# A second block of the first expert moved from the loop to the stretch between attention and loop

## Chip, core and metric

The kernel runs on one core of a Trainium2 chip. The metric is the device time of one execution in microseconds. TensorE (PE) multiplies, ScalarE (ACT) and VectorE (DVE) work elementwise, GpSimd (POOL) does elementwise work and issues indirect DMAs, SyncE (SP) issues the other DMAs. Every engine works through its own instructions in order and waits on semaphores for the others.

## The reference

```
attn: q, k, v (8, 8, 576, 64); k and v are averaged over runs of 8 rows (72 left)
      out = softmax(q kp^T / sqrt(64)) vp
x     = attn as (4608 tokens, 512)
moe:  expert = argmax(x @ w_gate) of 8; p = softmax probability of that expert
      y[token] = p * (relu(x @ w1[expert]) @ w2[expert]),  w1 512x1024, w2 1024x512
```

The tokens are grouped by their expert, each expert's tokens go through its two matrices, and the rows go back to their places.

## The kernel before

**Attention in units.** The 4608 tokens are 36 units of 128 tokens. Each unit is transposed, multiplied, exponentiated and normalised; units form seven groups (6, 6, 6, 6, 6, 4, 2). When a group is done, `route` finds each token's expert and its place in an array in HBM, `x_by_expert`, which has one segment per expert. POOL then scatters the rows there, one indirect DMA for each unit (`scatter`). The lists `hooks` and `fillers`, written by hand, say what other work is put between the steps of which unit.

**Blocks of the experts.** An expert's tokens are taken in blocks of 256 rows. All numbers are kept as pairs of fp16, a high and a low part. For one block the steps are: load the rows (`load_x`), split them into high and low (`split_x`, ACT makes the high part, DVE the low one), let the DMA transpose them into the buffer `xTs` (`turn` in two pieces, `trans` in one), copy them to `xT` on DVE (`arrive`), eight steps `up(s, f, n)` of 12 matmuls each into PSUM tiles `ps`, `ps`, `pp` (two f for each 128x512 tile), `relu_hi` (ACT) and `relu_lo` (DVE) into the buffers `bd`, four times 12 matmuls `finish(s, j, half)` into `pY[j]`, `take(j)` (ACT, times the token's probability), and `give(j)` (POOL, an indirect DMA to the output). `keep_ids`, `move_ids` and `take_ids` pass a block's token numbers and probabilities through three pairs of small buffers on POOL; `keep_ids` also overwrites the numbers in the row buffer by the mark `far`.

**The early block.** Behind the third group of units a count of the first expert's tokens is compared with 256 (`okf`). If there are that many, `early_load` at unit 29 loads the first block into `xg`; POOL splits it (`split_early` at unit 30), `turn` follows at unit 31, and the first three `up` steps are put into units 33 to 35 (`UPAT`).

**Between attention and loop.** The other `up` steps follow, and between them lie the counts of all experts (`counted`), the last group's scatters and the table of the blocks (`ended`, `table`, `tables`). `table` says for each round of the loop where its rows lie, which weight buffers it uses, and how many rounds there are (`T`). Then come `finish`, the loading and splitting of the loop's first two blocks (`xg`, `xg2`), `take` and `give`.

**The loop.** `For_i(0, T)` does one block a round (`block`). The x of the next rounds is loaded, split and transposed one and two rounds ahead. Weights of the next expert are split by ACT and DVE (`wsplit` in `part`) in the first round and in each expert's first round. Code for the four cases (weight buffers 0 or 1, 256 or 128 rows) stands one behind the other, and every engine jumps to the case that the table names.

Of the kernel before, what the change touches and what calls it, by code (L numbers as in the profile page):

```python
# [9 lines left out]
F32 = mybir.dt.float32  # L10
F16 = mybir.dt.float16
# [21 lines left out]
def kernel(  # L33
# [169 lines left out]
    for e in range(E):  # L203
# [12 lines left out]
    hT = [x.rearrange("p (f t) -> p f t", f=FC) for x in bd[0:2]]  # L216
    xh = bd[2].rearrange("p (j a x) -> p j a x", j=2, a=2)
    ys = [x.rearrange("p h d -> p (h d)") for x in ql]
    xg, xg2 = (VB[i].rearrange("p y c s x -> p (y c s x)").bitcast(F32)[:, 0:2 * XW]
               .rearrange("p (j x) -> p j x", j=2) for i in (2, 0))  # L220

    def blank_x(x):
        nc.gpsimd.memset(x, 0.0)
# [383 lines left out]
    def route(gidx):  # L607
# [103 lines left out]
        def early_pe():  # L711
            pm = psA.tile([128, 512], F32, name="pq", bufs=2)
            nc.tensor.matmul(pm[:, 0:1], ones, Z["c16"][:, 0:1], start=True, stop=True)
            V.tensor_scalar(okf, pm[:, 0:1], 256.0, None, op0=OP.is_ge)

        def early_int():
            V.tensor_copy(oki, okf[0:1, :])
# [89 lines left out]
    def put(i, pos, f, *a):  # L807
        assert 0 <= i < NU
        hooks.setdefault((i, pos), []).append((f, a))
# [94 lines left out]

    def early_load():
        assert KVS.pop("early") and not any(g < EARLY for g, _, _ in pend)
        KVS["ok"] = nc.values_load(oki[0:1, 0:1], engines=[ENG.SP], min_val=0, max_val=1)
        with tc.If(KVS["ok"] > 0):
            ld = nc.sync.dma_start(xg, xs[0:BLK, :].rearrange("(j p) x -> p j x", p=128))
        for o in scat[bounds[EARLY][0]:]:  # L910
            tc.declare_no_dep(ld.ins, o.ins, reason="rows of other tokens")
        soon.append(ld)

    put(28, "sp", blank_x, xg)
    put(29, "sp", early_load)

    def first_block():
# [102 lines left out]
    def relu_hi(k):  # L1020
        nc.scalar.activation(hT[0][:, 2 * k:2 * k + 2, :].rearrange("p f t -> p (f t)"), pH[k], AF.Relu)  # L1021
# [15 lines left out]
    pH += [pp[:, 0:512], pp[:, 512:1024]]  # L1037
    pY = [psA.tile([128, 2, 512], F32, name="po")[:, 0, :]]
    rest = [f for _, _, f in fillers]
    for x in range(max(len(front), len(rest))):  # L1040
        for f in (front[x:x + 1] + rest[x:x + 1]):
            f()
# [6 lines left out]
    def counted():  # L1049
        pc = pq["pc"] = psA.tile([128, 512], F32, name="pq", bufs=2)  # L1050
        nc.tensor.matmul(pc[:, 0:E], ones, c16, start=True, stop=True)
        rank()
        lt = pq["lt"] = work.tile([128, E], F16, name="lt")
        V.tensor_tensor(lt, pc[:, 0:E], thr, op=OP.is_gt)
        V.tensor_copy(pads, pc[0:1, 0:E])
        for x in range(2):
            h = slice(64 * x, 64 * x + 64)
            V.tensor_scalar(padi[h], pc[h, 0:E].rearrange("p (c x) -> p c x", x=2)[:, :, x], pio[h], None, op0=OP.add)
        pcs = pq["pcs"] = work.tile([128, E], F32, name="pcs")
        V.tensor_copy(pcs, pc[:, 0:E])  # L1060
        for e in range(n0 + n1):
            eng, et = ((nc.sync, ENG.SP), (nc.scalar, ENG.Activation))[e >= n0]
            r = nc.values_load(pads[0:1, e:e + 1], engines=[et], min_val=e * SEG, max_val=e * SEG + SEG - 128)
            padded.append((e, sent(eng.dma_start(xs[ds(r, 64), :], zpad[0:64]))))
# [73 lines left out]
    for f in range(FC):  # L1138
        if f >= len(UPAT):
            up(0, f, BLK)  # L1140
        if f + 1 == 5:
            counted()
        if f + 1 == 6:
            ended()
        if f + 1 == 8:
            tables()
        if f in (1, 3):
            relu_hi(f // 2)
    for k in (2, 3):
        relu_hi(k)  # L1150
    for k in range(4):
        relu_lo(k)
    views = [x.rearrange("p a b c -> p (a b c)") for x in qt] + [x.rearrange("p c x -> p (c x)")[:, 0:2048] for x in kv[1:]]
    views = [x.bitcast(F16) for x in views]
    W1[1] = [x.rearrange("p (c f) -> p c f", c=DC) for x in views[:2]]
    W2[1] = [x.rearrange("p (c f) -> p c f", c=FC) for x in views[2:]]
    pY.append(psA.tile([128, 512], F32, name="pq", bufs=2))
    for j, half in ((1, 0), (1, 1), (0, 0), (0, 1)):
        finish(0, j, half)

    def entry(kind, t, engines, lo, hi):
        ap = tabs[kind:kind + 1, t:t + 1] if isinstance(t, int) else tabs[kind:kind + 1, ds(t, 1)]
# [20 lines left out]
                with tc.If(many > 1):  # L1183
                    part(128, 64, x[0:64, 1])

    xh2 = kv[1].rearrange("p c x -> p (c x)")[:, 0:1024].bitcast(F16).rearrange("p (j a x) -> p j a x", j=2, a=2)
    blank_x(xg2)
    load_x(0)
    load_x(1, xg2)
    wlate(1)  # L1190
    for j in range(2):
        x, h = xg[:, j, 0:Dm], xh[:, j]
        nc.scalar.activation(h[:, 0], x, AF.Copy)
        V.tensor_tensor(h[:, 1], x, h[:, 0], op=OP.subtract)
    keep_ids()
    move_ids()
    turn()
    load_x(2)
    split_x(xg2, xh2)
    keep_ids(xg2)  # L1200
    trans(xh2)
    with tc.If(nc.values_load(tab[0:1, 1:2], engines=[ENG.Activation, ENG.DVE, ENG.SP], min_val=0, max_val=1) > 0):
        for j in range(8):
            wsplit(1, j)
        wwhole(2, 1)
        wwhole(3, 0)
    T = nc.values_load(tab[0:1, 0:1], min_val=1, max_val=TMAX)

    given = []

    def take(j):
# [2 lines left out]
    def give(j):  # L1214
# [6 lines left out]
            tc.declare_no_dep(st.ins, o.ins, reason="rows of other tokens")  # L1221
        given.append(st)

    take(1)
    give(1)
    take(0)
    give(0)

    def part(s, en):
        with tc.If(en > 0):  # L1230
# [76 lines left out]
```

## Time and profile before

| | us |
|---|---|
| median of 3 runs (lowest, highest) | 645.96 (644.94, 652.38) |
| profiled execution, its time | 643.61 |
| its span in the trace | 641.8 |
| PE busy | 579.4 |
| DVE, ACT, POOL busy | 335.2, 287.2, 278.2 |

The profiled execution takes 1.8 us beside its span, and it lies 2.35 us under the median of the three runs. Times in the rows below are microseconds from the start of the span. An engine's idle time stands in brackets with what released it.

### The profile page before, as it was taken

What the parts mean: (1) busy time and instruction counts of PE and PEld (TensorE: products, weight loads), DVE (VectorE), ACT (ScalarE), POOL (GpSimd) and SP (SyncE); (2) the same over time, 40 slices, a digit from 0 to 9 for tenths busy, and PEclk for the clock granted to TensorE, in tenths of its full rate; (3) what the DMA queues carried; (4) which work ended last, traced back from release to release, by engine and by line L of the source; (5) the groups of instructions that cost most, each with busy time, mean ns of one, the idle gap of its engine ahead of it and who ended that gap; (6) DMA issues with size and microseconds to landing.
All of it is one profiled execution on the core that took longest, in us unless ns stands there. A gap on an engine that the chain in (4) does not pass through costs nothing. (4 is left out here: it accounts for less than half of the span.)

```text
span 641.8 us, 15925 instructions
## 1 busy us (share of the span) xinstructions
PE 579.4 (90%) x4694; PEld 425.7 (66%) x4695; DVE 335.2 (52%) x683; ACT 287.2 (45%) x630; POOL 278.2 (43%) x531
## 2 busy tenths in 40 slices
PE   6888788888879788998899999999999989999995
PEld 5877677777758364675566677666667666677663
DVE  7577888898897417221864655213631272221212
ACT  2576676777752216221763644223622262221222
POOL 6799599798795522112125033213031232012212
PEclk9798999998989979998999999999999999999998
DMA  8997769965667774963389397633212323213200
GB/s 241 291 288 228 212 190 276 286 200 172 200 159 279 201 125 109 392 196 83 101 269 342 90 326 225 206 75 86 51 49 81 93 69 98 49 49 82 65 16 31
DMA packets 104204, 105.63 MB, mean 165 GB/s; under 512 B 62310, under 2 KB 72550, under 8 KB 104168
## 3 DMA queue, kind: packets, MB, share of 16 engines
q1 hardware_dynamic: 97528, 85.46, 47.9%
q0 software_dynamic: 6640, 19.71, 8.4%
q8 instruction: 20, 0.33, 0.2%
q14 instruction: 16, 0.13, 0.1%
HBM read 71.77 MB, written 22.06 MB: 146 GB/s over the span
## 5 line engine op out<-in xcount | busy, mean ns | idle before, releaser
L1031 PEld LDWEIGHTS <-bd 128*128 128x128 f16 x936 | 91.3, 98 | 105.7 <-ACT bd L1021 0.8
L1216 POOL TENSOR_TENSOR spacer<-ql,iG 1x1 f32<-1x1 f32 x44 | 23.8, 541 | 218.0 <-ACT ql L1212 217.0
L1025 DVE SCALAR_TENSOR_TENSOR bd<-ps,bd 128x512 f16<-128x512 f32 x44 | 30.1, 690 | 150.2 <-ACT bd L1021 150.1
L504 ACT ACTIVATE both<-ps,nmx 128x72 f32<-128x72 f32 x288 | 68.7, 325 | 32.8 <-DVE nmx L497 32.4
L1025 DVE SCALAR_TENSOR_TENSOR bd<-pp,bd 128x512 f16<-128x512 f32 x44 | 30.3, 691 | 100.6 <-ACT bd L1021 100.6
L1021 ACT ACTIVATE bd<-pp 128x512 f16<-128x512 f32 x44 | 26.2, 598 | 108.9 <-PE pp L961 78.8
L1021 ACT ACTIVATE bd<-ps 128x512 f16<-128x512 f32 x44 | 26.1, 597 | 75.8 <-PE L959 68.6
L1031 PE MATMUL po<-w,bd 128*128 128x512 f16 x264 | 58.8, 379 | 0.0
L1031 PE MATMUL po<-kv,bd 128*128 128x512 f16 x264 | 58.8, 379 | 0.0
L959 PE MATMUL ps<-kv,w 128*128 128x256 f16 (+1 forms) x176 | 44.0, 263 | 10.2 <-DMA kv<-bd 7.3
L1217 POOL DMA_INDIRECT out_dram<-ql,iG x44 | 43.8, 995 | 21.7 <-issue 20.2
L959 PE MATMUL ps<-kv,qt 128*128 128x256 f16 (+1 forms) x176 | 46.4, 268 | 4.9 <-issue 3.5
L487 PE MATMUL ps<-bd,qT 128*128 128x144 f32 x256 | 47.9, 314 | 3.2 <-DMA bd<-bd 1.6
L545 PE MATMUL po<-vb,ph 128*128 128x146 f16 (+2 forms) x384 | 33.7, 233 | 18.1 <-DVE l L586 7.3
L1031 PE MATMUL pq<-kv,bd 128*128 128x512 f16 x216 | 48.1, 379 | 0.0
L961 PE MATMUL ps<-kv,qt 128*128 128x256 f16 (+1 forms) x176 | 46.4, 268 | 1.9 <-DVE qt L116 1.9
L960 PE MATMUL ps<-kv,qt 128*128 128x256 f16 (+1 forms) x176 | 46.4, 268 | 0.0
L961 PE MATMUL ps<-kv,w 128*128 128x256 f16 (+1 forms) x176 | 44.0, 263 | 2.5 <-DVE w L116 2.5
L959 PEld LDWEIGHTS <-w 128*128 128x128 f16 x352 | 34.7, 99 | 15.7 <-issue 10.4
L960 PE MATMUL pp<-kv,qt 128*128 128x256 f16 (+1 forms) x176 | 44.7, 263 | 0.0
L961 PE MATMUL pp<-kv,qt 128*128 128x256 f16 (+1 forms) x176 | 44.7, 263 | 0.0
L959 PE MATMUL pp<-kv,qt 128*128 128x256 f16 (+1 forms) x176 | 44.7, 263 | 0.0
(235 smaller groups left out, 1374.6 us busy)
## 6 DMA issues: line engine op xcount, KB each, us to landing
both<-in_moe_w_dram SPq DMA_DIRECT2D x6, 2048.0 KB, 11.1
st<-in_moe_w_dram SPq DMA_DIRECT2D x6, 2048.0 KB, 13.4
vb<-x_by_expert SPq DMA_DIRECT2D x17, 514.0 KB
st<-in_moe_w_dram SPq DMA_DIRECT2D x8, 1024.0 KB
kv<-in_k_dram SPq DMA_DIRECT2D x7, 1024.0 KB
kv<-in_v_dram SPq DMA_DIRECT2D x7, 1024.0 KB
qt<-in_q_dram SPq DMA_DIRECT2D x6, 1024.0 KB
qt<-in_q_dram SPq DMA_DIRECT2D x4, 512.0 KB
```

Source lines behind the costliest of these rows:

```text
L487: nc.tensor.matmul(ps[:, x * 2 * KP:(x + 1) * 2 * KP], t[:, h, :], BD[b % 3][:, :, h, :], start=True, stop=True)
L504: nc.scalar.activation(p[:, h * KP:(h + 1) * KP], ps[:, x * KP:(x + 1) * KP], AF.Exp, bias=nmx[:, x:x + 1], scale=-1.0)
L545: nc.tensor.matmul(po[:, half, cols], a[:, c * 128:(c + 1) * 128], VB[b % 3][:, y, c, sl, 0:CW], start=st, stop=False, skip_group_check=True)
L959: nc.tensor.matmul(dst, wh, xT[:, d, 0:n], start=(d == 0), stop=False)
L960: nc.tensor.matmul(dst, wh, xT[:, DC + d, 0:n], start=False, stop=False)
L961: nc.tensor.matmul(dst, wl, xT[:, d, 0:n], start=False, stop=(d == DC - 1))
L1021: nc.scalar.activation(hT[0][:, 2 * k:2 * k + 2, :].rearrange("p f t -> p (f t)"), pH[k], AF.Relu)
L1025: V.scalar_tensor_tensor(l, pH[k], 0.0, h, op0=OP.max, op1=OP.subtract)
L1031: nc.tensor.matmul(y, hT[x][:, f, 128 * j:128 * j + 128], W2[s][z][:, f, :], start=(half == x == z == f == 0), stop=(half == z == 1 and f ...
L1216: nc.gpsimd.tensor_tensor(spacer[:, 0:1], ys[j][0:1, 0:1], iG[0:1, j:j + 1].bitcast(F32), op=OP.add)
L1217: st = nc.gpsimd.indirect_dma_start(out=out, out_offset=bass.IndirectOffsetOnAxis(ap=iG[:, j:j + 1], axis=0), in_=ys[j], in_offset=None, b ...
```

## The change

A second block of 256 rows of the first expert is worked through ahead of the loop.

- `early_pe` adds a comparison with 512, so that `okf` is 0, 1 or 2; the table starts at that block and the loop runs that many rounds fewer.
- `xg2` and its split `xh2` are both put into `kv[1]`. `early_load` makes two guarded loads, `blank_x(xg2)` moves from behind the pads to unit 28.
- `relu_hi(0)` and `relu_lo(0)` stand ahead of the last groups' `route` steps; the other relus follow pair by pair behind f = 3, 5 and 7.
- Behind the units the second block is split on ACT and DVE, transposed (`trans(xh2)`) and copied (`arrive`). `counted`, `ended` and `tables`, which stood between the `up` steps, now stand between the four `finish` steps, behind `arrive`.
- Then `take` and `give` of the first block, the second block's `up`, relu and `finish` steps, and between them loading, splitting and transposing of the loop's first two blocks.

```
-            V.tensor_scalar(okf, pm[:, 0:1], 256.0, None, op0=OP.is_ge)
+            V.tensor_scalar(okf, pm[:, 0:1], float(BLK), None, op0=OP.is_ge)
+            V.scalar_tensor_tensor(okf, pm[:, 0:1], 2.0 * BLK, okf, op0=OP.is_ge, op1=OP.add)
...
+        for n, x in enumerate((xg, xg2)):
+            with tc.If(ok > n):
+                ld = nc.sync.dma_start(x, xs[n * BLK:(n + 1) * BLK, :].rearrange("(j p) x -> p j x", p=128))
...
     put(28, "sp", blank_x, xg)
+    put(28, "sp", blank_x, xg2)
...
+    relu_hi(0)
+    relu_lo(0)
     for x in range(max(len(front), len(rest))):
...
-        if f + 1 == 5:
-            counted()
-        if f + 1 == 6:
-            ended()
-        if f + 1 == 8:
-            tables()
-        if f in (1, 3):
+        if f in (3, 5, 7):
             relu_hi(f // 2)
-    for k in (2, 3):
-        relu_hi(k)
-    for k in range(4):
-        relu_lo(k)
+            relu_lo(f // 2)
+    split_x(xg2, xh2)
+    keep_ids(xg2)
+    move_ids()
+    trans(xh2)
+    arrive()
...
+    finish(0, 0, 0)
+    counted()
+    finish(0, 0, 1)
+    ended()
     pY.append(psA.tile([128, 512], F32, name="pq", bufs=2))
-    for j, half in ((1, 0), (1, 1), (0, 0), (0, 1)):
-        finish(0, j, half)
+    finish(0, 1, 0)
+    tables()
+    finish(0, 1, 1)
...
+    take(0)
     take(1)
     give(1)
+    give(0)
+    take_ids()
+    load_x(0)
+    load_x(1, xg2)
+    for h in range(2):
+        for f in range(4 * h, 4 * h + 4):
+            up(0, f, BLK)
+        for k in (2 * h, 2 * h + 1):
+            relu_hi(k)
+            relu_lo(k)
+    split_x()
+    keep_ids()
+    move_ids()
+    trans()
+    for half in range(2):
+        finish(0, 1, half)
+    arrive()
+    load_x(2)
+    split_x(xg2, xh2)
+    keep_ids(xg2)
+    trans(xh2)
+    take(1)
+    give(1)
+    for half in range(2):
+        finish(0, 0, half)
     take(0)
     give(0)
```

Two places show what moves on the engines. The lines of the changed kernel are numbered a little higher (L1030 there is L1025 before).

DVE before, behind the last group's `route` steps: `c16` is cast from the running counts `cum`, and the counts' own work (`lt`, `pads`, `padi`, `pcs`, then `rt`) follows at once.

```order
L705 TENSOR_TENSOR cum<-cum,rso 128x8
L1044 CAST c_3434<-cum 128x8
L1054 TENSOR_TENSOR lt<-pq,thr 128x8
L1055 CAST pads<-pq 1x8
L1058 TENSOR_SCALAR padi<-pq,pio 64x4 x2
L1060 COPY pcs<-pq 128x8
L669 TENSOR_TENSOR rt<-pq,roh 128x16
```

Nothing stands between the cast and the counts. DVE after, the same place: L1030 is `relu_lo`, L894 the low half of `split_x`, L905 `arrive`.

```order
L707 TENSOR_TENSOR cum<-cum,rso 128x8
L1051 CAST c_3441<-cum 128x8
L1030 SCALAR_TENSOR_TENSOR bd_160<-ps,bd_159 128x512
L1030 SCALAR_TENSOR_TENSOR bd_160<-pp,bd_159 128x512 x2
L894 TENSOR_TENSOR kv_153<-kv_153 128x2x512
L905 COPY kv_131<-kv_131 128x2x8x128
L1061 TENSOR_TENSOR lt<-pq,thr 128x8
L1062 CAST pads<-pq 1x8
L1065 TENSOR_SCALAR padi<-pq,pio 64x4 x2
L1067 COPY pcs<-pq 128x8
L671 TENSOR_TENSOR rt<-pq,roh 128x16
```

Three relus, the split and `arrive` now stand between the counts' cast and the work on the counts.

SP before, at unit 29: the flag `oki` is read, one guarded load of the early block (L909) follows, then the moves (L1006) of the last image's value rows.

```order
L907 TENSOR_LOAD oki
L907 ISA x2
L908 COMPARE_AND_BRANCH
L909 DMA vb_164<-x_by_expert 128x2x514
L908 UNCONDITIONAL_BRANCH x2
L1006 DMA vb_163<-vc 40x2x72
L1006 DMA vb_163<-vc 32x2x72
```

The first of eight moves stands right behind the one load. SP after, the same place:

```order
L910 TENSOR_LOAD oki
L910 ISA x2
L912 COMPARE_AND_BRANCH
L913 DMA vb_164<-x_by_expert 128x2x514
L912 UNCONDITIONAL_BRANCH x2
L912 COMPARE_AND_BRANCH
L913 DMA kv_153<-x_by_expert 128x2x514
L912 UNCONDITIONAL_BRANCH x2
L1011 DMA vb_163<-vc 40x2x72
```

A second guarded load stands ahead of the moves.

On POOL, `keep_ids(xg2)` and `move_ids` now stand between the fifth and the sixth scatter of the fifth group. The mark `far` in `keep_ids` waits for the low half of the split on DVE, and the last seven scatters and the pads stand behind it.

## Rows read from the trace of the kernel before

**Rows 1.** The profile's page: busy time (share of the span, instructions) of each engine.

```profile
PE 579.4 (90%) x4694; PEld 425.7 (66%) x4695; DVE 335.2 (52%) x683; ACT 287.2 (45%) x630; POOL 278.2 (43%) x531
...
L1021 ACT ACTIVATE bd<-pp 128x512 f16<-128x512 f32 x44 | 26.2, 598 | 108.9 <-PE pp L961 78.8
```

**Rows 2.** The timeline of PE from the last units to the second round of the loop: start, duration, engine, line, operation, tiles, count, and in brackets the idle time ahead of it with its releaser.

```profile
201.74 0.27 PE L959 MATMUL ps<-kv,w 128*128 128x256 f16 x1
203.05 0.27 PE L959 MATMUL pp<-kv,w 128*128 128x256 f16 x1
...
205.24 0.17 PE L1051 MATMUL pq<-c,ones 128*128 128x8 f16 x1 [0.72 <-DVE c L1044]
...
209.36 0.27 PE L961 MATMUL pp<-kv,w 128*128 128x256 f16 x1
...
210.77 5.34 PE L1031 MATMUL pq<-w,bd 128*128 128x512 f16 x24
215.95 5.34 PE L1031 MATMUL po<-w,bd 128*128 128x512 f16 x24
227.40 0.37 PE L959 MATMUL ps<-kv,w 128*128 128x256 f16 x1 [6.11 <-DMA kv<-bd]
...
239.85 5.34 PE L1031 MATMUL pq<-w,bd 128*128 128x512 f16 x24
245.03 5.34 PE L1031 MATMUL po<-w,bd 128*128 128x512 f16 x24
253.21 0.27 PE L959 MATMUL ps<-kv,w 128*128 128x256 f16 x1 [2.83 <-DVE kv L116]
...
263.69 5.34 PE L1031 MATMUL pq<-w,bd 128*128 128x512 f16 x24
```

**Rows 3.** Busy time in stretches: stretch, its length, busy us (and instructions) of PE, PEld, DVE, ACT, POOL, the granted clock of PE as a share of full speed, the DMA share and GB/s.

```profile
202.00:206.00 4.00, 3.28 (x35) 2.80 (x33) 3.56 (x23) 1.19 (x3) 1.53 (x3) 1.00 0.35 134
...
226.00:230.00 4.00, 2.60 (x13) 1.84 (x14) 0.00 (x0) 0.00 (x0) 1.99 (x6) 0.50 0.57 93
...
300.00:304.00 4.00, 4.00 (x48) 4.00 (x46) 0.69 (x1) 1.04 (x2) 0.20 (x1) 0.61 0.02 4
```

**Rows 4.** Unit 28 to 33: SP's guarded load of the early block (its branches: shortest, median, longest in ns, first and last start), the moves behind it and the two transposes, in the DMA queue of SP; POOL's blanking and the end of its split; PE's waits in the same units.

```profile
L908 SPq COMPARE_BRANCH  x2: 38/45/52, 174.8 to 175.7; - x2
```

```profile
175.87 6.63 SPq L1006 DMA_DIRECT2D vb<-vc  x8
184.13 2.76 SPq L895 DMA_TRANSPOSE kv<-bd  x2
```

```profile
172.36 0.98 POOL L223 MEMSET vb<- 128x1028 f32 x1
...
182.04 2.06 POOL L886 TENSOR_TENSOR bd<-vb,bd 128x1024 f16<-128x1024 f32 x1
```

```profile
183.46 1.73 PE L545 MATMUL po<-vb,ph 128*128 128x146 f16 x12 [3.09 <-issue]
...
192.66 0.27 PE L959 MATMUL ps<-kv,w 128*128 128x256 f16 x1 [1.16 <-DMA kv<-bd]
```

**Rows 5.** The timeline of DVE behind the units (counts, table, relus), and the same kinds of work in the loop's first round.

```profile
204.95 0.24 DVE L1044 CAST c<-cum 128x8 f16<-128x8 f32 x1
205.44 0.17 DVE L1054 TENSOR_TENSOR lt<-pq,thr 128x8 f16<-128x8 f32 x1 [0.26 <-PE pq L1051]
...
206.25 0.17 DVE L669 TENSOR_TENSOR rt<-pq,roh 128x16 f32<-128x16 f32 x1
...
210.41 0.14 DVE L1130 TENSOR_TENSOR tab<-pq,okf 1x1 int32<-1x1 f32 x1
...
211.07 1.26 DVE L1025 SCALAR_TENSOR_TENSOR bd<-ps,bd 128x512 f16<-128x512 f32 x2
```

```profile
243.03 0.68 DVE L902 COPY kv<-kv 128x2048 f16<-128x2048 f16 x1
243.63 1.22 DVE L891 TENSOR_TENSOR bd<-vb,bd 128x1024 f16<-128x1024 f32 x1
```

**Rows 6.** The timeline of ACT in the loop's first round: the high half of the split.

```profile
242.25 1.06 ACT L890 ACTIVATE bd<-vb 128x1024 f16<-128x1024 f32 x1
```

**Rows 7.** The transposes of whole blocks by their line, 20 of them in the loop and ahead of it, first all, then the one issued at 245.0 alone: time from issue to landing.

```profile
DMA to landing us min/median/max: 4.3/4.3/12.0
```

```profile
DMA to landing us min/median/max: 6.0/6.0/6.0
```

**Rows 8.** POOL's last scatters of rows, by their line from 190 to 215 and the last one in the timeline, and the load of the loop's first two blocks on SP that waits for them.

```profile
L694 POOL DMA_INDIRECT x_by_expert<-both,rpos x12: 959/963/1037, 191.7 to 210.6; - x12
...
DMA to landing us min/median/max: 3.0/7.0/8.2
```

```profile
210.59 0.96 POOL L694 DMA_INDIRECT x_by_expert<-both,rpos  x1 [0.23 <-issue]
```

```profile
215.40 3.00 SPq L1171 DMA_DIRECT2D vb<-x_by_expert  x2
```

```profile
221.29 1.15 ACT L1193 ACTIVATE bd<-vb 128x512 f16<-128x512 f32 x2 [10.54 <-DMA vb<-x_by_expert]
```

**Rows 9.** The branches of PE's sequencer at the cases of the loop's body, at the entry into the loop and behind its first block.

```profile
L1252 PEldq COMPARE_BRANCH  x2: 71/87/103, 219.8 to 219.9; - x2
```

```profile
L1252 PEldq COMPARE_BRANCH  x3: 71/93/4866, 246.3 to 253.0; - x3
```

More of the change, by code (lines that the diff above doesn't have):

```diff
@@ L218 @@
     ys = [x.rearrange("p h d -> p (h d)") for x in ql]
-    xg, xg2 = (VB[i].rearrange("p y c s x -> p (y c s x)").bitcast(F32)[:, 0:2 * XW]
-               .rearrange("p (j x) -> p j x", j=2) for i in (2, 0))
+    xg, xg2 = (x.rearrange("p (j x) -> p j x", j=2)
+               for x in (VB[2].rearrange("p y c s x -> p (y c s x)").bitcast(F32)[:, 0:2 * XW],
+                         kv[1].rearrange("p c x -> p (c x)")[:, 1024:1024 + 2 * XW]))
+    xh2 = kv[1].rearrange("p c x -> p (c x)")[:, 0:1024].bitcast(F16).rearrange("p (j a x) -> p j a x", j=2, a=2)
     def blank_x(x):
@@ L906, in early_load @@
         assert KVS.pop("early") and not any(g < EARLY for g, _, _ in pend)
[L907 to L912, printed above, removed]
+        ok = nc.values_load(oki[0:1, 0:1], engines=[ENG.SP], min_val=0, max_val=2)
+        for n, x in enumerate((xg, xg2)):
+            with tc.If(ok > n):
+                ld = nc.sync.dma_start(x, xs[n * BLK:(n + 1) * BLK, :].rearrange("(j p) x -> p j x", p=128))
+            for o in scat[bounds[EARLY][0]:]:
+                tc.declare_no_dep(ld.ins, o.ins, reason="rows of other tokens")
+            soon.append(ld)
     put(28, "sp", blank_x, xg)
+    put(28, "sp", blank_x, xg2)
     put(29, "sp", early_load)
@@ L1184, in load_x @@
                     part(128, 64, x[0:64, 1])
[L1186 to L1207, printed above, removed]
     given = []
@@ L1222, in give @@
         given.append(st)
+    take(0)
     take(1)
     give(1)
+    give(0)
[23 more added lines that the diff above has]
+        finish(0, 0, half)
     take(0)
     give(0)
+    with tc.If(nc.values_load(tab[0:1, 1:2], engines=[ENG.Activation, ENG.DVE, ENG.SP], min_val=0, max_val=2) > 0):
+        for j in range(8):
+            wsplit(1, j)
+        wwhole(2, 1)
+        wwhole(3, 0)
+    T = nc.values_load(tab[0:1, 0:1], min_val=1, max_val=TMAX)
     def part(s, en):
```

## The prediction

> **What bounds the kernel now.** I read the busy times first: PE is busy for 579.4 of 641.8 us and no other engine passes 52% [rows 1], so only what PE does not do while it waits can be won. The same 22 blocks (44 relus of each second half, two for a block, [rows 1]) have to be done before and after; the change takes no matmul away. Next I read PE's timeline around the stretch that the change rewrites [rows 2]. One sees a small wait between the early block's steps (0.72 us), then 6.11 us without a matmul from 221.29 to 227.40, while the loop's first x is loaded, split and transposed, and 2.83 us ahead of the loop's second round. Last I read the stretches with PE's granted clock [rows 3]: it is 0.50 of full speed in 226 to 230, after the 6.11 us of idling. That is 1.2 instead of 2.4 GHz. The first round's eight steps take 12.45 us (227.40 to 239.85), against 10.48 in the second round (253.21 to 263.69). So the hole costs 6.1 and some 2.0 us: at most about 8 us lie there for the change to take, 1.3% of the time.
>
> The measure I use is the moment at which PE has done two blocks of the first expert: before, 245.03 + 5.34 = 250.37 [rows 2]. Everything behind it, the 2.83 us too, exists in both kernels.
>
> **Part 1, the units.** SP makes a second guarded load at unit 29. One such load takes from the first branch at 174.8 to the last at 175.7, 0.9 us [rows 4]; the eight moves behind it (to 182.50) start 0.9 us later, and PE's wait of 3.09 us at 183.46 ends with their landing. POOL blanks a second buffer, 0.98 us and a small mark, ahead of its split of the first block, whose end at 184.10 releases the transposes at 184.13, for which PE waits 1.16 us at 192.66 [rows 4]. The two run side by side, so they don't add: I take 1.1 us later for all behind unit 31. Bounds: 0.3, if the moves have slack, and 2.0, if 514 KB more in the DMA queues push the moves back as well.
>
> **Part 2, the first block's steps.** `relu_lo(0)` (1.26 / 2 = 0.63 us, [rows 5]) stands ahead of the routing on DVE: the cast of the counts, done at 205.19, is done at 205.19 + 1.1 + 0.63 = 206.9. Behind it come `relu_lo` 1 and 2, to 208.2. Steps f = 3 to 5 take PE to 201.74 + 1.1 + 3 x 1.31 = 206.8; step f = 6 waits in the changed order for `relu_lo(2)`, which reads the other half of its PSUM tile, so it starts at about 208.3 and f = 7 ends at 208.3 + 2.62 = 210.95. Before it was 209.63. The 0.72 us of waiting for the counts are gone, 1.5 us of waiting for a relu have come.
>
> **Part 3, the new chain behind the steps.** PE goes on with the first two `finish` steps: 24 matmuls, 5.18 us (210.77 to 215.95, [rows 2]), to 216.3. Meanwhile, from 211.1: `relu_hi(3)` 0.60 (the mean of its group, [rows 1]), split high 1.06 [rows 6], split low 1.22 [rows 5] to 214.0, transpose, then `arrive` 0.68, then five small DVE operations on the counts (205.44 to 206.23, 0.8 us). These used to be hidden under `up` steps. Now `arrive` stands ahead of them, so DVE, and with it the counts, the table and PE's next matmul of `ended`, wait for a DMA. The transpose's landing is the term that I can't read: 4.3 us in the median, 6.0 for the one at 245.0 [rows 7], and 8.5 for the two pieces at unit 31 (184.13 to the 192.66 at which PE goes on, [rows 4]), in full queues. The DMA share is down to 0.35 from 202 to 206 [rows 3] and the new transpose comes at 214, so it is nearer to the first two: I take 5.5 and keep 4.3 and 8.5 as ends. That gives 214.1 + 5.5 + 0.7 + 0.8 = 221.1. PE idles from 216.3 to 221.1, 4.8 us: most of the hole is not gone but moved.
>
> Then the table: from `rt` to its end DVE takes 206.25 to 210.55, 4.3 us [rows 5]. It may also wait for the fifth group's last scatter, which POOL now issues only behind the split (`keep_ids`): 214.9 + 7.0 [rows 8] = 221.9, some 0.4 us more. So the table's transpose is at 221.1 + 4.3 + 0.4 = 225.8. Under this lies the third `finish` step, 2.6 us at full clock and 5.2 at half; after 4.8 us of idling I expect half clock for most of it, as in the rows with 0.50, so it ends at about 226. That costs nothing as long as the table takes longer. The fourth step and the transpose end at 229.0.
>
> **Part 4, the second block.** Its `up` steps need only `xT`, there since 220.3; `take(1)` frees the PSUM tile at about 230, 10 us before it is written again. A block takes 10.48 for its `up` steps and 2 x 5.18 for `finish`, 20.84 us, so it ends at 249.9. Against 250.37 that is 0.5 us won. The loop's x is now hidden: the seven held scatters, some 1.3 us apart (0.96, 0.23 idle and a memset), are issued by about 224.5 and land by 232.7 at the latest (8.2 us); then the load may go, and takes 5.9 us (215.40 to 221.29, [rows 8]), to 238.6. It is split behind the second block's relus, from 242. Its transpose can start 4.9 us behind the last `up` step (239.85 to 243.63 + 1.22, a little less since `arrive` stands ahead there, [rows 2, 5]), and with 4.3 us landing and 0.7 us `arrive` the loop could go on after 9.9 us, with 6.0 us after 11.6. PE's `finish` steps cover 10.4. So the loop starts 0 to 1.2 us late; I take 0.6.
>
> **Sum.** -0.5 + 0.6 = +0.1 us: the profiled 643.61 would be 643.7. The profile stands 2.35 us under the median of the runs, so I add the change to the median: 645.96 + 0.1, **646 us**, no change. A measurement of this kernel tells about 2%, 13 us, from no change; this is far inside.
>
> Later rounds keep their distances: the first expert has one round less between the loading of the third expert's weights (behind the first round) and their split, but even behind the slowest transpose, 12.0 us [rows 7], I count 2 to 3 us to spare, so I put nothing down.
>
> **Rivals.** *Faster.* The transpose lands in 4.3 us (-1.2), the scatter is not waited for (-0.4), the loop's first x comes in time (-0.6), and the clock, which fell to 0.61 in 300 to 304 in the fourth round [rows 3], does not fall there (4 us at 0.61 lose 1.5): 646 - 3.7 = 642.3. For it speaks that most transposes take 4.3; against it that all four must hold.
>
> *Slower, by the transpose.* POOL holds seven scatters back until the split is done and then issues them with the transpose in flight; before, the line's last twelve were spread over 191.7 to 210.6 [rows 8]. One transpose took 12.0 us to land [rows 7]. Each us of landing over 5.5 is a us of PE. With 8.5 the time is 646 + 3 = 649, with 12.0 652.5. It decides as soon as the landing passes 5.4 us, the point of no gain.
>
> *Slower, by the entry into the loop.* PE's sequencer spent 4.87 us on one branch behind the first block, its first jump over the other cases, and PE idled 2.83 us there; at the entry the same line took 0.07 to 0.10 us [rows 9]. Before, the entry lay under the 6.11 us hole; now PE arrives with work ready. If the first jump stalls as the other did, the time is 646 + 2.8 = 648.8. Against it: the entry's branches were short. The Trainium skill (Runtime: NRT & Kernel Launch, section Instruction fetch mechanics) says that a taken branch whose target is not among the instruction blocks held makes the engine wait for a fetch. By that rule the row with 4866 ns is such a fetch, and the time would be that of this rival; the entry's row shows none.
>
> *It does not do what it says.* If the first 18 units held fewer than 512 tokens of the first expert, an empty block would be worked through and the loop run 21 rounds: 646 + 20.8 = 667. From the reference with its inputs I count 1016 there, so this needs a fault.
>
> **How the numbers follow.** Forecast 646, with 643.5 to 648 as its own range: 0.50. Faster rival 0.18, slow transpose 0.22, loop entry 0.08, no second block 0.02. The range from 642 to 651 reaches to the middle of the faster and over most of the slow cases; left out are some 0.05 below and 0.1 above, and the spread of single runs. Over 2% faster would need more than the hole holds: 0.01. Over 2% slower needs the empty block or several queues jammed at once: 0.03. The rest, 0.96, is within 2%.
>
> **What would show it.** In the profile after, PE should have an idle time of 4 to 6 us ahead of the eight small matmuls of `ended`, released by DVE, with `arrive` just ahead of the counts on DVE and the transpose's landing ahead of that; half clock in the `finish` step behind it; step f = 6 released by DVE about 1.5 us late; the wait at unit 31 about 4 us instead of 3.09; no 6 us hole ahead of the loop; 2.8 us behind its first round as before; 20 rounds. The prediction is wrong if the idle time ahead of `ended` is under 2 us or over 8, or if the second block's first `up` step starts outside 226.5 to 232.

## The result

| | changed / before | 95% interval | changed, before: median us |
|---|---|---|---|
| first measurement | 1.0075 | 1.0049 to 1.0100 | 653.28, 649.85 |
| second | 1.0060 | 1.0032 to 1.0088 | 653.16, 648.86 |
| third | 1.0027 | 0.9996 to 1.0059 | 659.24, 656.65 |

The forecast was 646.0 us, between 642 and 651, and no change. The first measurement, which it is held against, gave 653.28 us: outside the range. By the medians the changed kernel is 2.6 to 4.3 us slower, by the ratios 1.8 to 4.9; the third interval still takes in no change at all. The medians leave out runs that lie more than 1.5% above the fastest of their kernel. The median of the kernel before stands at 649.85 in 20 runs, not at the 645.96 of the three runs from which the forecast set out. From one measurement to the next it goes from 648.86 to 656.65.

The profiled execution of the changed kernel takes 654.81 us, its span 652.8. Its page begins as follows. PE's busy time is up by 7.0 against [rows 1], and matmuls at half clock are a part of that; the last line is the granted clock, in 40 slices of the span:

```profile
PE 586.4 (90%) x4694; PEld 430.8 (66%) x4695; DVE 333.9 (51%) x684; ACT 286.2 (44%) x629; POOL 276.0 (42%) x531
...
PEclk9698998989889889999999999999999989999998
```

PE's timeline, its first step of each stretch and its waits, to be read beside [rows 2] and [rows 4]:

```profile
188.97 0.48 PE L547 MATMUL po<-vb,ph 128*128 128x146 f16 x2 [2.17 <-issue]
190.16 0.19 PE L547 MATMUL po<-vb,ph 128*128 128x73 f16 x1 [0.72 <-DMA vb<-vc]
...
192.04 0.95 PE L547 MATMUL po<-vb,ph 128*128 128x73 f16 x7 [0.55 <-DMA vb<-vc]
...
200.03 0.27 PE L964 MATMUL ps<-kv,w 128*128 128x256 f16 x1
...
214.61 0.27 PE L964 MATMUL pp<-kv,w 128*128 128x256 f16 x1 [1.41 <-DVE bd L1030]
...
227.16 0.35 PE L1092 MATMUL pq<-lt,ones 128*128 128x8 f16 x8 [4.49 <-DVE pcs L1067]
227.37 5.01 PE L1036 MATMUL pq<-w,bd 128*128 128x512 f16 x12
...
234.92 0.27 PE L964 MATMUL ps<-kv,w 128*128 128x256 f16 x1
...
257.21 0.28 PE L964 MATMUL ps<-kv,w 128*128 128x256 f16 x1 [1.29 <-ACTq L1274]
...
281.01 0.27 PE L964 MATMUL ps<-kv,w 128*128 128x256 f16 x1 [2.79 <-DVE kv L116]
...
306.36 0.22 PE L964 MATMUL ps<-kv,qt 128*128 128x128 f16 x1 [4.34 <-issue]
```

The 6.11 us hole is gone and in its place 4.49 us ahead of `ended`, 1.41 ahead of step f = 6 and 1.29 at the loop's entry. At unit 31 PE waits 2.17, 0.72 and 0.55 us, 3.4 in all. The last row is new: `ps<-kv,qt` is the first block of the second expert, the fifth of all, whose weights lie in `qt`. PE waits 4.34 us there. In the kernel before the same row reads:

```profile
297.89 0.22 PE L959 MATMUL ps<-kv,qt 128*128 128x128 f16 x1 [2.85 <-issue]
```

To see where the two kernels part I cut the span at the first `up` steps of the blocks (us; other profiles of both kernels, see the experiments, stand beside the first ones):

| stretch | before, 1st | 2nd | 3rd | changed, 1st | 2nd |
|---|---|---|---|---|---|
| start to first block | 192.66 | 192.66 | 200.64 | 200.03 | 198.99 |
| first to second block | 34.74 | 44.01 | 39.51 | 34.89 | 34.77 |
| second to third | 25.81 | 23.77 | 23.83 | 22.29 | 22.29 |
| third to fifth | 44.68 | 44.48 | 46.35 | 49.15 | 49.24 |
| fifth to seventh | 37.44 | 38.98 | 37.88 | 39.17 | 39.69 |
| seventh to the end | 306.47 | 310.70 | 310.09 | 307.27 | 308.82 |

The first two rows differ by 8 and 9 us from one execution of the kernel before to the next, so nothing of the change can be read there from single profiles. From the second block to the seventh the profiles of one kernel lie close together: 107.93, 107.23 and 108.06 before, 110.61 and 111.22 after. I take these 3.2 us for the change's. They are of the same size as the difference of the medians, but what the change adds or saves in the first two rows stays unknown.

### The profile page after: what moved, and what is told of

Its sections match the earlier page's. It is cut to its first block, busy times and chain, and to the rows that moved or that the text cites. A ratio compares the mean times of both kernels' runs of the same rounds, so it can differ in the third digit from the quotient of the medians.

```text
span 652.8 us, 15798 instructions
## 1 busy us (share of the span) xinstructions
PE 586.4 (90%) x4694; PEld 430.8 (66%) x4695; DVE 333.9 (51%) x684; ACT 286.2 (44%) x629; POOL 276.0 (42%) x531
## 5 line engine op out<-in xcount | busy, mean ns | idle before, releaser
L1030 DVE SCALAR_TENSOR_TENSOR bd<-ps,bd 128x512 f16<-128x512 f32 x44 | 30.2, 689 | 148.2 <-ACT bd L1026 148.2
L1030 DVE SCALAR_TENSOR_TENSOR bd<-pp,bd 128x512 f16<-128x512 f32 x44 | 30.4, 691 | 103.5 <-ACT bd L1026 103.5
L489 PE MATMUL ps<-bd,qT 128*128 128x144 f32 x256 | 49.5, 322 | 3.5 <-DVE L L590 1.3
L1036 PE MATMUL pq<-w,bd 128*128 128x512 f16 x192 | 45.1, 393 | 0.0
```

What stands on the lines that cost most here:

```text
L489: nc.tensor.matmul(ps[:, x * 2 * KP:(x + 1) * 2 * KP], t[:, h, :], BD[b % 3][:, :, h, :], start=True, stop=True)
L1030: V.scalar_tensor_tensor(l, pH[k], 0.0, h, op0=OP.max, op1=OP.subtract)
L1036: nc.tensor.matmul(y, hT[x][:, f, 128 * j:128 * j + 128], W2[s][z][:, f, :], start=(half == x == z == f == 0), stop=(half == z == 1 and f ...
```

## The experiments

**The changed kernel and the kernel before, once more.** No edit. 

> The changed kernel itself, once more, beside the kernel before on the same chip. If the result of 1.0075 is right: 1.005 to 1.010 again, and the profile shows again 4.5 us ahead of the matmuls of ended, 1.3 us at the loop's entry and a longer stall at the third expert round's jump (4.3 us against 2.8). What of the first profile was spread (the 4.9 us ahead of unit 26, the 2.4 us of the units, the extra half clock at 324 and 529 us) comes out at other sizes.

Measured: 1.0060 (1.0032 to 1.0088). The waits come out again: 4.08 us ahead of `ended`, 1.29 at the loop's entry, 4.38 at the second expert.

> The kernel before itself, profiled a second time. It tells which numbers of the two profiles differ from one execution to the next: the first up step's place (192.66 us in the first profile of before, 195.5 to 200.6 in the kernels with the second early load) and the stretches at half clock. If the 7.4 us between the first up steps are mostly spread, the first up step stands at 195 us or later here; if they are the change's, at 191 to 194.

Measured: one run, 656.43 us, span 654.6. The first `up` step stands at 192.66 again, under the 195 that spread would have needed; a third profile, below, has it at 200.64. So its place alone tells nothing. PE's timeline of this second profile of the kernel before has two waits that the first one lacks (the last row is the first step of the second block):

```profile
201.73 1.65 PE L545 MATMUL po<-vb,ph 128*128 128x146 f16 x12 [4.54 <-ACT ph L513]
...
223.75 0.37 PE L1134 MATMUL pq<-ident,tf 128*8 128x128 f32 x1 [6.91 <-remote]
...
236.67 0.28 PE L959 MATMUL ps<-kv,w 128*128 128x256 f16 x1
```

The 6.11 us hole ahead of that block, from which the prediction set out, is not there: this row has no wait. PE idles 6.91 us ahead of the table's transpose instead. ACT stands idle earlier in the same stretch, where "remote" means that no event of the trace released it:

```profile
200.97 0.70 ACT L513 ACTIVATE ph<-pp 128x640 f16<-128x640 f32 x1 [6.69 <-remote]
```

> The changed kernel a third time, on the chip and at the time of the three others: 1.005 to 1.010 of the kernel before, if what was measured twice holds; nearer to 1.000 if the kernel before has in some of its sittings 6 us more ahead of the loop (its second profile) which the changed kernel hasn't.

Measured: 1.0027 (0.9996 to 1.0059). This is under the expected range and nearer to no change. The waits in its profile are the same at the loop's entry (1.28 us) and at the second expert (4.34).

> The kernel before against itself: 1.000 within its interval. Its profile tells whether it has the 6 us more between first up step and loop, which the second profile showed and the first did not (table 13 us late, ACT and DVE idle with nothing in the trace that they wait for).

Measured: 0.9961 (0.9932 to 0.9991). The kernel before against itself differs by 0.4%, with an interval that does not hold 1; the expectation missed. So an effect of less than half a per cent is not settled by one such ratio. That the changed kernel is the slower one rests on three of them and on the table above. The waits of 2.69 (for ACT's `ph`) and 6.93 us ("remote") stand in this profile too, and again there is no hole ahead of the second block: this holds for two of three profiles of the kernel before.

**The units alone.** 

> The kernel before with the first part of the change alone: at unit 28 a second buffer is blanked, at unit 29 a second guarded load of 256 rows follows the first; nothing reads it. The prediction's term: first up step 1.1 us later (bounds 0.3 to 2.0), the time up by 1.1 us. Rival A (the traces of before and after): about 2.4 us, because the longer waits around unit 31 also cost some more us at half clock; the time up by 2 to 3 us. Rival B: the 2.4 us between the two traces is the spread between executions, and the time rises by under 0.5 us.

```
+        for n, x in enumerate((xg, xz)):
+            with tc.If(KVS["ok"] > 0):
...
+    put(28, "sp", blank_x, xz)
```

Measured: 0.9973 (0.9931 to 1.0015), that is -4.5 to +1.0 us. The interval leaves out the 2.4 us that lay between the two first profiles, and the prediction's 1.1 us lie just past its edge; but a kernel against itself gave 0.9961, so neither is settled. PE's waits at unit 31 add up to 2.18 + 0.61 + 0.88 + 0.63 = 4.3 us in this profile, against 3.09 [rows 4], 3.4 and 3.4 in the three profiles of the kernel before. No loss shows in the time.

**The second load later.** 

> The changed kernel with the blank of the second buffer at unit 30 (behind the split of the first block) and its load at unit 32 (behind the moves and the transposes). If the units term is 2.4 us, the time falls by about 2 us against the changed kernel (653.3 to 651), and the wait of PE at unit 31 is back at about 3.1 us. By the prediction's own term the time falls by 1.1. If the lag of the units is spread alone: no change against the changed kernel. The idle time ahead of the counts' matmuls stays at 4 to 5 us in all cases.

```
...
-    put(28, "sp", blank_x, xg2)
+    put(30, "sp", blank_x, xg2)
+    put(32, "sp", load_early, 1, xg2)
```

Measured: 1.0007 (0.9972 to 1.0043), at another time than the changed kernel; against the 1.0027 to 1.0075 of that one it may be worth up to 4 us or nothing. PE's wait at unit 31 is 0.77 us, far under the expected 3.1, and the 4.48 ahead of `ended` are there as expected.

**The counts ahead of the copy.** 

> The changed kernel with the counts behind step f = 5, ended behind the split of the second block and ahead of its transpose, and arrive behind the four finish steps. Theory: PE no longer waits for the transpose, since four finish steps (10.4 us) cover its landing (5.5 us) and arrive. The idle time of 4.5 us ahead of the counts goes, and with it some us of half clock: 4 to 6 us less than the changed kernel, 647.5 to 649.5, at or a little below the kernel before. Rival: the table or the scatters are late instead, PE waits at the third or fourth finish step, and less than 2 us is won. Second rival: the loop's entry takes the gain back with a longer wait.

```
+        if f == 5:
+            counted()
     split_x(xg2, xh2)
+    ended()
     keep_ids(xg2)
     move_ids()
     trans(xh2)
-    arrive()
...
     finish(0, 0, 0)
-    counted()
     finish(0, 0, 1)
-    ended()
...
     finish(0, 1, 1)
+    arrive()
```

Measured: 0.9946 (0.9913 to 0.9978). PE's timeline from `ended` to the second block's first step, and at the second expert:

```profile
216.32 0.34 PE L1092 MATMUL pq<-lt,ones 128*128 128x8 f16 x8
216.53 5.34 PE L1036 MATMUL po<-w,bd 128*128 128x512 f16 x24
...
302.12 0.27 PE L964 MATMUL ps<-kv,qt 128*128 128x128 f16 x1 [6.26 <-issue]
```

No wait is left ahead of `ended` and no half clock behind it (24 matmuls in 5.34 us, against 12 in 5.01). The second block starts 30.68 us behind the first instead of 34.89: the 4.2 us of the theory. But PE now waits 6.26 us at the second expert. The second rival was right in kind: the gain was in part taken back, one jump later than it said.

**Both.** 

> Both edits in one: late load and blank, and counts ahead of the transposed copy. If the terms add: 6 to 8 us less than the changed kernel, 645.5 to 647.5, and 2 to 4 us less than the kernel before. If the gain of the one is given back at the loop's entry or in the first jump over code, it is no faster than the kernel before.

Measured: 0.9863 (0.9803 to 0.9924) and, at another time, as the fourth kernel:

> The fourth kernel (late load, counts ahead of the copy) beside the split-early kernel on the same chip: 0.983 to 0.99 of the kernel before again. PE's first branch to the second expert's code takes 8 to 10 us, its wait there 6 to 8 us.

0.9950 (0.9916 to 0.9983). The branch took 9.9 us and PE's wait 8.2 in the first profile, 6.0 and 4.29 in the second. The ratio lies above the expected range and the stall below it. So that stall differs from one execution to the next.

**What the stall at the second expert is.** The rows of PE's branches at the jump to the second expert's code (shortest, median, longest in ns), first in the kernel before, then in the changed kernel:

```profile
L1252 PEldq COMPARE_BRANCH  x3: 189/375/3406, 291.0 to 294.2; - x3
```

```profile
L1269 PEldq COMPARE_BRANCH  x3: 203/363/6012, 298.0 to 300.1; - x3
```

One branch takes 3.4 us before and 6.0 after. What else runs there is seen on SP. The loads of the third and fourth expert's weights (L87, four of 2 MB each) in the kernel before and in the changed one:

```profile
252.25 2.27 SPq L87 DMA_DIRECT2D both<-in_moe_w_dram  x2
255.55 5.83 SPq L87 DMA_DIRECT2D st<-in_moe_w_dram  x2
```

```profile
279.30 3.30 SPq L87 DMA_DIRECT2D both<-in_moe_w_dram  x2
283.46 6.45 SPq L87 DMA_DIRECT2D st<-in_moe_w_dram  x2
```

They follow the loop's first round. Before, two more blocks lie between that round and the second expert (some 42 us), now one (21 us, since a block of the loop has become an early one). The stretches tell how full the queues are (the last three columns are granted clock, DMA share and GB/s), before and after, each around its own jump:

```profile
286.00:290.00 4.00, 4.00 (x20) 1.84 (x19) 2.70 (x4) 1.61 (x2) 0.11 (x1) 1.00 0.00 0
290.00:294.00 4.00, 4.00 (x20) 1.78 (x19) 0.00 (x0) 0.69 (x1) 1.38 (x3) 1.00 0.84 178
294.00:298.00 4.00, 1.15 (x7) 0.42 (x5) 0.00 (x0) 0.69 (x1) 1.34 (x4) 1.00 0.32 83
298.00:302.00 4.00, 3.92 (x37) 3.20 (x36) 0.23 (x1) 0.60 (x1) 1.01 (x7) 0.72 0.21 72
```

```profile
294.00:298.00 4.00, 4.00 (x21) 1.80 (x19) 2.42 (x3) 1.61 (x2) 0.14 (x1) 1.00 1.03 420
298.00:302.00 4.00, 4.00 (x19) 1.63 (x17) 0.00 (x0) 0.00 (x0) 1.24 (x3) 1.00 1.04 403
302.00:306.00 4.00, 0.01 (x1) 0.00 (x0) 0.00 (x0) 0.69 (x1) 1.81 (x6) 1.00 1.26 368
306.00:310.00 4.00, 3.59 (x31) 2.86 (x32) 0.00 (x0) 0.27 (x1) 0.00 (x0) 0.63 1.02 185
```

Around the long branch the DMA share is 0.32 in the kernel before (294 to 298) and 1.04 to 1.26 in the changed one (298 to 306).

**Without the loads.** 

> The changed kernel without the loads of weights inside the loop: the experts from the third on are multiplied by old numbers in the staging buffers; all else runs as in the changed kernel. If the full queues make the branch slow: PE's branch at the jump to the second expert falls from 6.0 to 3.4 us or less and the wait behind it from 4.3 to 2.8 us or less. If not: 6.0 and 4.3 us as before. The end of the first round keeps its 2.8 us in both cases, since nothing is loaded there yet.

```
-        for x in (0, 1):
-            with tc.If(en3[x] > 0):
-                wwhole(en3[x], 1 - x)
```

The branch and the wait behind it:

```profile
L1269 PEldq COMPARE_BRANCH  x3: 208/362/3012, 293.3 to 296.4; - x3
```

```profile
299.69 0.22 PE L964 MATMUL ps<-kv,qt 128*128 128x128 f16 x1 [2.37 <-issue]
```

One run, 646.54 us. 3.0 and 2.37 us are what the theory has: with nothing else changed ahead of that place, the loads in flight make the branch 3.0 us longer and the wait 2.0.

What the branch waits for stands in the trace too. Two of the DMA queues are of the kind `instruction`, and the packets of one of them, q8, hold 16 KB. The trace does not say for which engine they are. But PE has two long branches in each of the eighteen profiles (before, after and the experiments), and 35 of these 36 have exactly one packet of q8 inside them, the other has two. The queues of the changed kernel (packets, MB, share of the engines), first from the branch's start at 300.07 to 303.60, then from there to 304.70:

```profile
q1 hardware_dynamic: 602, 1.23, 93.7%
q0 software_dynamic: 39, 0.16, 11.4%
```

```profile
q1 hardware_dynamic: 165, 0.34, 78.8%
q0 software_dynamic: 39, 0.09, 21.5%
q8 instruction: 1, 0.02, 6.1%
```

The packet comes 3.5 us behind the branch's start. Without the loads it comes 0.7 us behind it (from 296.41 to 297.07, then to 298.02):

```profile
q0 software_dynamic: 19, 0.01, 4.5%
```

```profile
q8 instruction: 1, 0.02, 6.1%
```

At the second expert the packet starts 0.6 to 1.1 us behind the branch's start in the ten profiles whose queues are free of the weights, and 3.5 to 6.8 us behind it in the eight with the loads in flight. From the packet's start to the branch's end it is 2.3 to 3.1 us in all eighteen. So what the loads lengthen is the wait for the instruction packet.

> The changed kernel without the loads of weights inside the loop (the experts from the third on use old numbers), timed in rounds: its one run was 6.6 us under the changed kernel's median. If the loads in flight cost what the profiles showed from the third block to the seventh (142 against 146 us from the first up step to the seventh block): 3 to 5 us less than the changed kernel, 0.998 to 1.002 of the kernel before.

Measured: 0.9976 (0.9946 to 1.0005) beside 1.0027 for the changed kernel on the same chip, by the medians 4.0 us less (655.24 and 659.24); the two intervals overlap by a little. The branch took 3.3 us there, the wait 2.70. From the second block to the seventh the two profiles without the loads take 107.12 and 109.57 us, against 110.61 and 111.22 with them. In the second one PE runs at a granted clock of 0.65 from 278 to 282, behind the jump at the end of the first round, so the 2.0 us of the shorter wait are not all seen there.

**The loop's entry.** 

> The changed kernel without take(0) and give(0) of the second early block ahead of the loop: 128 rows of the output are not written there. If PE's 1.3 us at the loop's entry are ACT coming to the loop late, behind take(0), which waits for PE's last finish step: the wait falls under 0.5 us. If it is PE's own entry (its branches or register loads): 1.3 us as before.

```
-    take(0)
-    give(0)
     with tc.If(nc.values_load(tab[0:1, 1:2], engines=[ENG.Activation, ENG.DVE, ENG.SP], min_val=0, max_val=2) > 0):
```

```profile
253.16 0.27 PE L964 MATMUL ps<-kv,w 128*128 128x256 f16 x1 [0.86 <-DVEq L1272]
```

0.86 instead of 1.29, released by DVE instead of ACT: between the two expectations. ACT was late behind `take(0)`, but only by 0.4 us; next is DVE's own entry. In the kernels below, which lack the guarded block ahead of the loop with its register load on both engines, the wait is 0.67.

**The weights split and loaded ahead of the loop.** 

> The fourth kernel (late load, counts ahead of the copy) and beside that the second expert's weights are split on ACT and DVE between attention and loop, in the gaps of the second block's relus, and the loads of the third and fourth expert's weights (8 MB) are issued ahead of the loop instead of behind its first round; the loop's first round splits no weights. Theory (the queues are full of these 8 MB when PE takes its first jump to the other expert's code, so its branch takes 6 to 10 us instead of 3.4): the loads are done some 20 us ahead of the jump, the branch takes 3.5 us or less, PE waits at most 3 us there instead of 8.2, and the wait of 2.85 us at the end of the loop's first round goes too: 5 to 8 us less than the fourth kernel, 0.975 to 0.98 of the kernel before. Rival: the branch's time has nothing to do with the loads; it stays at 6 to 10 us, and only the 2.85 us are won. Second rival: the splits hold the second block's relus up on ACT and DVE and PE waits there.

```
+    for j in (0, 1):
+        wsplit(1, j)
     finish(0, 0, 0)
...
     arrive()
+    for j in (2, 3, 4, 5):
+        wsplit(1, j)
...
+        if h == 0:
+            for j in (6, 7):
+                wsplit(1, j)
...
+    trans(xh3)
+    wwhole(2, 1)
+    wwhole(3, 0)
```

The guarded block ahead of the loop, which held splits and loads, goes; the table of the blocks no longer asks for a split in the loop's first round; and the loop's second x has buffers of its own (`xg3`, `xh3`). Measured: 0.9862 (0.9818 to 0.9905), 641.76 us. The expected 0.975 to 0.98 was missed: at another time the fourth kernel had 0.9863. Beside the fourth kernel:

> The split-early kernel on the same chip as the fourth. From the first up step to the end of the sixth block its profile was 9.9 us shorter than the fourth's (136.75 against 146.66). If that is what the earlier loads give: 6 to 10 us less than the fourth kernel, 0.972 to 0.978 of the kernel before. If the fourth's long stall is a rare case and its usual one is like the changed kernel's 4.3 us: 3 to 5 us less than the fourth.

0.9881 (0.9835 to 0.9926) beside 0.9950: 4.5 us less by the ratios and 6.7 by the medians, the lower of the two expectations or just above it. The branch at the second expert is down to 3.2 and 3.4 us in the two profiles, PE's wait to 2.45 and 2.71. But the loads are now in flight when PE takes its jump at the end of the first round, and that branch rose from 4.9 to 5.7 us, its wait to 3.69 and 3.59, in place of the 2.85 for the splits.

**One load ahead, one behind.** 

> The split-early kernel, with only the third expert's weights (4 MB) loaded ahead of the loop and the fourth's behind its first round. If the full queues stretch each first jump (5.7 against 4.9 us at the end of the first round in the split-early kernel, 6 to 10 against 3.0 to 3.4 us at the second expert): now both come in queues that are empty of weights, the branch at the first round's end is back at 4.9 us, its wait at 2.8 instead of 3.7 us, and the second expert's stays at 3 to 3.4 us: 1 to 2 us less than the split-early kernel. Rival: the second load (268 to 280 us) reaches the other jump and the gain is lost there.

```
-    wwhole(3, 0)
+    with tc.If(nc.values_load(tab[0:1, 1:2], engines=[ENG.SP], min_val=0, max_val=2) > 0):
+        wwhole(3, 0)
```

The fourth expert's load is back behind the first round, by the table. Both jumps in PE's timeline:

```profile
275.19 0.37 PE L971 MATMUL ps<-kv,w 128*128 128x256 f16 x1 [2.83 <-issue]
...
300.47 0.22 PE L971 MATMUL ps<-kv,qt 128*128 128x128 f16 x1 [2.78 <-issue]
```

Measured: 0.9868 (0.9828 to 0.9909). The waits are as expected, 2.83 and 2.78, and the branches 4.87 and 3.45 us. In the time it can't be told from the kernel with both loads ahead (647.03 and 647.61 us).

**The split alone in the changed kernel.** 

> The changed kernel and only this beside it: the second expert's weights are split between attention and loop (six pieces behind the last finish step of the first block, two between the second block's relus), the third and fourth expert's weights are loaded ahead of the loop. Early load, counts and transposed copy stay where the changed kernel has them. If the loads in flight at the jump to the second expert are what the changed kernel lost its gain to: the branch falls from 6.0 to 3.0 to 3.5 us, the wait of 2.85 us at the first round's end for the splits goes or is replaced by the branch's 3 to 3.7 us, and the time is 3 to 5 us less than the changed kernel: 0.998 to 1.002 of the kernel before. If the loss is in the units or in the wait ahead of ended: no more than 1.5 us less, 1.004 to 1.006.

Measured: 1.0025 (0.9989 to 1.0060), where the changed kernel had 1.0027. By the medians 1.6 us less (657.65 and 659.24), by the ratio nothing. In the profile the second expert's branch is 3.46 us and its wait 2.76, but the first round's branch is 5.7 and its wait 3.68, and PE runs at half clock behind that:

```profile
280.00:284.00 4.00, 4.00 (x25) 2.92 (x23) 0.27 (x1) 0.60 (x1) 0.00 (x0) 0.62 1.03 133
```

The third block to the fifth takes 51.14 us (49.15 and 49.24 in the changed kernel), the fifth to the seventh 37.95 (39.17 and 39.69). A part of the loss was moved from one jump to the other: by the waits alone 1.6 us go and 0.9 come. The half clock ate the rest here, but it is not a mark of this kernel. The changed kernel without its last `take` has it at the same place, behind a wait of 2.77 us:

```profile
276.00:280.00 4.00, 3.07 (x17) 2.27 (x18) 1.64 (x2) 0.00 (x0) 3.19 (x5) 0.57 0.86 300
```

The expectation missed: it counted the stall that goes and not the one that comes. Why the time shows nothing of the 0.7 us between them and of the shorter entry (0.67 us) stays open.

## Why the prediction failed

**What held.** Step f = 6 waits 1.41 us (1.5 in the prediction). The transpose lands 5.4 us behind its issue (220.26 to 225.69; 5.5 taken between 4.3 and 8.5):

```profile
225.69 0.73 DVE L905 COPY kv<-kv 128x2048 f16<-128x2048 f16 x1 [5.46 <-DMA kv<-kv]
226.34 0.15 DVE L1061 TENSOR_TENSOR lt<-pq,thr 128x8 f16<-128x8 f32 x1
```

PE idles 4.49 us ahead of `ended` (4.8). The `finish` step behind it runs at half clock (granted clock 0.50 from 226 to 230). The hole was moved, not filled. From its first `up` step to the end of the second block the changed kernel takes 55.89 us, the first profile of before 57.71: 1.8 won, where Part 4 without the units has 1.6. That the two agree is in part luck, since it holds for this pair of profiles alone: the other two of the kernel before take 65.0 and 60.5 us there, and have no hole ahead of the second block. The second block starts at 234.92, outside the 226.5 to 232 that I named as a sign of failure, but all of that lies ahead of the first `up` step, at 200.03 instead of 192.66, and there executions of the kernel before differ by 8 us as well. At unit 31 PE waits 3.4 us, where the prediction had about 4; the row of the 3.09 us names no releaser (`issue`), so that they end with the landing of the moves was its reading and not the row's. In Part 3, 221.9 lies 0.8 us and not 0.4 behind 221.1, which moves the sum by 0.2.

**The step that failed** is the sentence at the end of Part 4, that later rounds keep their distances, for which I put nothing down. I had seen that the third expert's weights now have one round less between their load and their split, and asked only whether the split would come late. It doesn't. But the same round less brings PE's first jump to the second expert's code into the load: 4.34 instead of 2.85 us of waiting, +1.5. The kernel without the loads loses this longer stall, the place of the instruction packet shows what it waits for, and the kernels with earlier loads show it move. From the fifth to the seventh block the changed kernel takes another 1.3 us (39.4 on the mean against 38.1), with the clock at 0.63 behind the longer idle time. What these 1.3 us are is not shown: without the loads the stretch takes 37.60 and 38.03, but with counts first and in the fourth kernel, whose waits are 6.26 and 8.20 us, it takes 37.97 and 38.10. Together that is 2.8 of the 3.2 us in the table. The entry's 1.29 us are nearly made up by half clock that two of the three profiles of the kernel before have between the second and the fourth block, 2.0 us of it in the first [rows 2].

**The rival that was nearest** is the entry into the loop with its first jump. It gave 648.8 by a stall of 2.8 us. The mechanism, a branch to code that isn't at hand, is the right one, and [rows 9] already held it. The place was wrong: at the entry PE's branches are short in the changed kernel too (0.07 to 0.11 us at the cases). Its wait there, 1.29 us, is not the late x for which the sum has 0.6: it is released by ACT, and 0.43 of it go with the last `take`. The Trainium skill (Runtime: NRT & Kernel Launch, section Instruction fetch mechanics) says that the target of such a branch is fetched by DMA before the engine goes on. The trace agrees: there is a packet of 16 KB inside every long branch. The branch at the second expert took 3.0 to 3.5 us with the weights' loads done or left out, and 6.0 to 9.9 with them in flight.

**The base was low,** and this is the larger part of the miss. I set the change on the median of three runs, 645.96, and knew that the profiled execution lay 2.35 us under it. Twenty runs have 649.85. Of the 7.3 us between 646.0 and 653.28, 3.9 are this and 3.4 the change. The range took in the costs of the change and only in passing the spread of single runs, which for this kernel is 8 us wide (643.8 to 652.38). With the base at 649.85 the time would have lain inside the range by a little; the forecast of no change would still have missed 3.4 us.

**What stays open.** Whether the units cost anything: one run bounds it to 1.0 us, which is about the prediction's term, and the 0.9961 of a kernel against itself makes that bound soft. What the 1.3 us from the fifth to the seventh block are. And what ACT and PE wait for between the last units and the table: the first two blocks of the kernel before lie 5 to 9 us further apart in two of its three profiles. In the second one the queues are full ahead of that stretch (DMA share 0.99 to 1.06 from 186 to 202), and the idle engines have no releaser. No run here shows that they wait for instructions: inside the 6.91 and 6.93 us ahead of the table neither of the two instruction queues in the trace moves a packet.

The kernel with both loads ahead (0.9862 and 0.9881) and the one with the loads apart (0.9868) beat both kernels, the kernel before by 7 to 9 us. They keep the second early block, put the counts ahead of the copy and move splits and loads; how much each edit gives is not told apart.

## What to carry to other kernels

When a change takes a round out of a loop, write down for every transfer of a round what it will now overlap, the fetch of code at the next untravelled case among it, and not only whether its data come in time. A step that waits for a DMA goes behind work that needs nothing from it: here the counts ahead of the transposed copy turned a loss of 0.3 to 0.75% into a gain of 0.5%. And before a forecast rests on one profile, look at how far the runs of the same kernel lie apart.

## What was not expected of the hardware

The first jump to the second expert's case costs PE a branch of 3.0 to 3.5 us with the queues free of the 8 MB of weights. With these loads in flight it costs 6.0 to 6.1 us in six profiles, 7.9 in the kernel with counts first and 9.9 in the fourth kernel's first profile. The jump at the end of the first round took 4.8 to 4.9 us in every kernel without such loads in flight, and 5.7 with them. The instruction packet inside it starts 2.6 to 2.7 us behind the branch's start, and 3.4 with the loads. So a transfer for whose data PE does not wait can still hold it up, by delaying the next packet of instructions.
